# Small matmuls of a chunked recurrence that alternate between the two column halves of the PE array, with the matmuls kept in program order to the end of the kernel

## The chip, the cores and the metric

The kernel runs on one core of a Trainium2 chip. The metric is device time in microseconds (us). Before the change it is 338.93 us, the median of three runs (337.6 to 339.09).

## The reference

Two layers stand one behind the other. The first is a linear recurrence over 768 positions for 4 batches of 8 heads (32 values of a head, 16 values of state), computed in chunks; a chunk's output has a part from the chunk itself and a part from the state that it was handed, and the chunk makes the next state. The second layer takes the 3072 rows of 256 values, forms `(x w1) * (x w2)` with 1024 columns, and multiplies by `w3` and `w_out`.

```python
cum = np.cumsum(la, axis=-1)                      # la: log a of this chunk
L = np.exp(cum[:, :, :, None] - cum[:, :, None, :]) * causal
M = np.einsum('bhin,bhjn->bhij', Cc, Bc) * L
y = M @ x + np.einsum('bhin,bhnd->bhid', Cc, state) * np.exp(cum)[..., None]
state = exp(sum(la)) * state + (B * x * decay_from_j).sum(positions)
...
a = x @ w1; b = x @ w2
out = (a * b @ w3) @ w_out
```

## The kernel before

**Chunks and slabs.** The positions are cut into 16 chunks of 48; two chunks make a slab, so there are eight slabs. A slab of all batches is 384 rows for the second layer. `w3 w_out` is formed once, at the start, into `WO`.

**One chunk of the recurrence** (`chunk(c)`) has four kinds of matmul, two heads to each. `decay` (tile `pd`) forms the exponents, ScalarE takes their exponential into `R`. `cb` (tile `pc`) forms the product of B and C: for the first slab two matmuls per half `hf` of the head pairs from float32 operands (tile `gf`), for every other slab 16 small bfloat16 matmuls per `hf`, 32 per chunk, of 96 rows, 64 columns and 48 streamed columns. `weigh` on VectorE multiplies `pc` into `R`. `Mx` (tile `py`) multiplies x and the state by `R`: 16 float32 matmuls of 128 rows, 64 columns and 64 streamed columns. The profile records a float32 matmul as two passes, so a `py` block is 32 passes, and a pass has its own weight load.

**Column halves.** The 64 columns of a small matmul lie either in PE columns 0 to 63 or in 64 to 127; which of them follows from the PSUM partitions that it writes (`64 * h2` in `cb`, `64 * pp` in `Mx`). Before the change the loop over the half is the outermost one: all matmuls of columns 0 to 63 first, then all of columns 64 to 127.

**After `Mx`** VectorE transposes the state out of `py` (`Z`), copies it with four small copies into the next chunk's operand `xe`, and ScalarE and VectorE write the outputs as two parts `xT` (high and low) for the second layer.

**The second layer** of a slab is eight tiles of `up` (tile `bank<-xT,w1..` and `w2..`: 12 matmuls with 384 streamed columns each), each followed by its gate: a copy on ScalarE, a product on VectorE (`gf`), a rounded copy on ScalarE (high part of `g`) and a difference on GpSimd (low part of `g`). Then come three groups of `down` (tile `bank<-woh,g` and `wol`: 24 matmuls with 256 streamed columns each, the eight tiles of `g` in turn, each with its high part twice and its low part last).

**What sets the order.** Slabs 0 and 1, the weights, and the chunks c0 to c5 are written out by hand in `PLAN`; there every instruction keeps the program's order. From slab 2 on (the loop at the end), `ordered[0]` is False and a scheduler decides, engine by engine; chunks c6 to c15 are formed there, two in each of the slabs 2 to 6, in four stages that are put behind the `up` tiles 0 to 3 (first chunk) and 4 to 7 (second chunk): `decay`, then `cb` and `weigh`, then `Mx`, then the steps after it.

Of the kernel before, what the change touches and what calls it, by code (L numbers as in the profile page):

```python
# [15 lines left out]
T = 48  # L16
# [4 lines left out]
PLAN = """  # L21
# [33 lines left out]
def kernel(  # L55
# [14 lines left out]
):  # L70
    """x, Bn, Bt, Ct, b0 and c0 as layouts() gives them, w3t with its columns first.
    The linear recurrence runs in chunks of T positions, two heads to a
    matmul.  The state rides along as N pseudo-positions in front of each
    chunk (their B rows are unit vectors, their x rows the state's rows), so
    one product M^T x gives the chunk's outputs with the carried part, and the
    columns B * decay beside M give the next state.  The layer (w3 w_out) is
    formed once.  float32 products of the layers go as hi + lo float32r parts, CB as
    sums over products of three bfloat16 parts."""
    nc = tc.nc
# [24 lines left out]

    # the start goes in the order of PLAN, engine by engine; the rest as it comes
    ordered = [True]

    def ins(i):
        return tc.keep_in_program_order(i) if ordered[0] else i

    def mm(*args, **kw):
        return ins(nc.tensor.matmul(*args, **kw))  # L112

# [14 lines left out]

# [1 line left out]
    # products of the two layers, by turns; before that the first slab's B^T  # L130
    # and C^T: rows (head pair of a half, n), columns (half, chunk, head
    # parity, ..), in C beside zeros for the other pairs' rows
    GF = const.tile([P, NGF, TOK], F32, name="gf")
# [14 lines left out]

    # exponent operands: rows 0..T-1 the causal mask, then per head parity three
    # parts of cum_i, then per head pair three parts of cum_j  # L150
    NG = NB * HP
# [13 lines left out]

# [1 line left out]
    Q, SQ = P // (NB * H), a.shape[1]  # L167
# [47 lines left out]

# [1 line left out]
    NQ = P // N  # L217
    XW = [t.shape[2] // NQ for t in (Bt, Ct)]
    dparts = [[dram.tile([3, N, NQ * XW[w]], BF16, name=f"d{'bc'[w]}{k}") for k in range(NSL)] for w in range(2)]

    # slots: B parts 0 1 2, 0 1, 0 against C parts 2 1 0, 1 0, 0; C's parts lie
    # in the order 2 1 0
    RUNS = ((0, 3, 0, 0), (3, 2, 0, 1), (5, 1, 0, 2))
# [61 lines left out]

# [1 line left out]
    xT = {}  # L287

    def chunk(c):
# [27 lines left out]
        def cb(hf):  # L317
            pc = ps_at.tile([P, 512], F32, name="pc", tag="at")
            pcv = v["pc", hf] = pc[:, :half * T].rearrange("p (g s) -> p g s", s=T)
            for h2 in range(2):  # L320
                if sl == 0:
                    kk = (hf * CPS + cc) * 2 + h2
                    mm(pcv[64 * h2:64 * h2 + 64].rearrange("p g s -> p (g s)"), B0[:, kk],
                       C0[:, kk].rearrange("p g t -> p (g t)"), start=True, stop=True)
                else:
                    for g in range(half):
                        mm(pcv[64 * h2:64 * h2 + 64, g], BP[:, hf * half + g, cc, h2], CP[:, hf * half + g, cc, h2],
                           start=True, stop=True)

# [4 lines left out]
        @step("Mx")  # L334
        def _():
            if cc == 0:
                xT[sl] = [work.tile([P, KT, NB, SL], F32R, name=f"xT{i}") for i in range(2)]
            py = ps_at.tile([P, 512], F32, name="py", tag="at")
            v["py"] = py.rearrange("p (k b m) -> p k b m", k=KT, b=NB)
            for pp in range(2):  # L340
                for kt in range(KT):
                    for b in range(NB):
                        hp = 2 * kt + pp
                        mm(v["py"][64 * pp:64 * pp + 64, kt, b, :], xe[:, b * HP + hp], v["R"][:, b * HP + hp, :],
                           start=True, stop=True)
# [35 lines left out]

# [1 line left out]
    W12 = [[const.tile([P, KT, DF], F32R, name=f"w{i}{p}") for p in "hl"] for i in (1, 2)]  # L383
    WO = [const.tile([P, FT, DM], F32R, name=f"wo{p}") for p in "hl"]

    def from_f64(name, src, dst=None):
        """Brings src, [P, 2 k] words of float64 in DRAM, low word first, to
        float32.  Scaled by 2^-112 as a float32, a high word has float32's
        exponent at its exponent's low end; magnitudes under 2^-119 vanish
        there.  Then the high word takes the low word's top byte as its lowest  # L390
        byte, to bring sign and last bits in one step."""
        v = {}

        @task(name + ".D")
        def _():
            v["st"] = work.tile([P, 2 * GR], F32, name="st", bufs=4)
            load(v["st"].bitcast(U32).rearrange("p (f k) -> p f k", f=src.shape[1]), src)
            v["wh"] = v["st"].rearrange("p (k two) -> p k two", two=2)[:, :, 1]

        @task(name + ".A")  # L400
        def _():
            v["mag"] = work.tile([P, GR], F32, name="mag", bufs=4)
            if name + ".A" in ON_VECTOR:
                ins(nc.vector.tensor_scalar(v["mag"], v["wh"], 2.0 ** -112, None, ALU.mult))  # L404
            else:
                ins(nc.scalar.activation(v["mag"], v["wh"], AF.Copy, scale=2.0 ** -112))

        @task(name + ".Y")
        def _():
            b = v["st"].bitcast(U8).rearrange("p (k e) -> p k e", e=8)  # L410
            (vcopy if name + ".Y" in ON_VECTOR else acopy)(b[:, :, 4], b[:, :, 3])

        @task(name + ".L")
        def _():
            w = v["wh"].bitcast(I32)
            ins(nc.vector.tensor_scalar(w, w, 5, 7 - 2 ** 31, ALU.arith_shift_right, ALU.bitwise_and))  # L416

        @task(name + ".S")
        def _():
            mi = v["mag"].bitcast(U32)  # L420
            to = mi if dst is None else dst.bitcast(U32)
            ins(nc.vector.scalar_tensor_tensor(to, mi, 3, v["wh"].bitcast(U32),  # L422
                                               ALU.logical_shift_left, ALU.bitwise_or))
        return v
# [11 lines left out]

    # the first WHOLE tiles of (w3 w_out)'s inner dimension go as float32 products
    WHOLE = 2
# [19 lines left out]
    def w3_item(j):  # L458
# [11 lines left out]
        @task(f"v{j}.M")  # L470
        def _():
            for b in range(f0 // 2, (f0 + NF) // 2):
                if b not in opened:
                    # the bank holds two accumulators: a product of zeros opens both
                    opened.add(b)
                    mm(bank[b], zero[:, 0:P], zero, start=True, stop=False)
            left[j % 2] -= 1
            for f in range(NF):
                ft = f0 + f
                fs = slice(f * P, (f + 1) * P)  # L480
                if kt < WHOLE:
                    pairs = [(v["mag"][:, fs], wof[:, kt])]
                else:
                    pairs = [(v["tr"][:, l, fs], wos[:, kt - WHOLE, r]) for l, r in ((0, 0), (0, 1), (1, 0))]
                for k, (l, r) in enumerate(pairs):
                    mm(bank[ft // 2][:, ft % 2, :], l, r, start=False,
                       stop=(left[j % 2] == 0 and k == len(pairs) - 1 and ft % 2 == 1))
# [11 lines left out]

# [1 line left out]
    turn = [0]  # L501
# [7 lines left out]
    def up(sl, ft):  # L509
        """(x w1) * (x w2) of one slab, one tile of columns"""  # L510
        hi, lo = [t.rearrange("p k b s -> p k (b s)") for t in xT[sl]]
# [60 lines left out]

# [1 line left out]
    for c in range(2 * CPS, 3 * CPS):  # L574
# [25 lines left out]
    def keep_clock(n):  # L600
        """products of zeros, for a tensor engine that would lose its clock waiting"""
        for _ in range(n):
# [61 lines left out]
def layouts(x, a, B, C):  # L664
    """a as [(quarter of the positions, head parity, batch, head pair), positions];
    x as [chunk, head parity, t, (batch, head pair, d beside zeros)]; B as [slab, (head
    parity, n's unit rows and t), (chunk, batch, head pair, n)]; B^T (behind
    unit columns) and C^T as [slab, n, (batch, head pair, chunk, head parity,
    t)]"""
    import numpy as np  # L670
# [18 lines left out]

    # the first slab's once more, as [(head pair of a half, n), (half, chunk, head parity, ..)]  # L690
    b0, c0 = [t[0].reshape(N, 2, G // 2, CPS, 2, -1).transpose(2, 0, 1, 3, 4, 5).reshape(N * G // 2, -1) for t in (bt, ct)]
# [36 lines left out]
```

## Time and profile before

| what | value |
|---|---|
| three runs | 337.6, 338.93, 339.09 us |
| span of the profiled execution, first to last instruction | 336.5 us |
| granted TensorE clock, mean over the core | 0.985 |
| TensorE (PE) busy | 306.7 us, 91% |
| VectorE (DVE), ScalarE (ACT), GpSimd (POOL) busy | 164.8, 153.1, 139.3 us |

The profile is of a further execution, whose span alone is known; the median of the runs is 2.4 us above it. In the profile PE is the matmul side of TensorE, PEld its weight loads, SPq the queue that issues DMAs. A row of the timeline gives the start, the length from the first start to the last end, engine, line, what is written from what, and how many instructions were merged; a bracket gives idle time ahead of them and what ended it. Matmuls are pipelined, so each record is longer than the distance to the next start. Since every matmul is issued through the helper `mm`, all of them have one line, L112, and are told apart by their tiles.

### The profile page before, as it was taken

Reading aid. Unit: us, or ns where it says so; the run is one execution under the profiler, and the core shown is the slowest. Engines: PE = TensorE matmul, PEld = TensorE weight load, DVE = VectorE, ACT = ScalarE, POOL = GpSimd, SP = SyncE. Lnnn points to the kernel's source line nnn. Section 1 sums busy time; section 2 is a strip of 40 time slices with the busy share of each in tenths; the row PEclk is TensorE's granted clock in tenths of the full one; section 3 lists DMA queues with packets and bytes.
Section 4 is the critical chain, followed back from the end, with each engine's and each line's share of the span. In section 5 each row is a group of like instructions: output and inputs, shape, how many; then the busy total and the mean of one; then the engine's idle time right before and its main releaser. Section 6 shows DMA issues by size and latency. Waiting matters only on the chain.

```text
span 336.5 us, 6661 instructions
## 1 busy us (share of the span) xinstructions
PE 306.7 (91%) x2569; PEld 276.7 (82%) x2571; DVE 164.8 (49%) x292; ACT 153.1 (45%) x290; POOL 139.3 (41%) x157
## 2 busy tenths in 40 slices
PE   8695896976868999899999999999999999999995
PEld 3452786965857998889999899889988998999995
DVE  3869989999987523634313340344035302510210
ACT  4466687866574644454214431433144223422421
POOL 8037278836856664243213421343043304420440
PEclk9799799799999999999999999999999999999999
DMA  7599699775969695753840294029302920001001
GB/s 210 186 285 266 213 261 231 231 226 159 299 155 190 209 208 185 237 150 85 174 101 20 52 179 95 19 82 179 76 8 60 196 56 3 2 2 47 0 2 47
DMA packets 26255, 45.31 MB, mean 135 GB/s; under 512 B 7600, under 2 KB 17200, under 8 KB 25552
## 3 DMA queue, kind: packets, MB, share of 16 engines
q1 hardware_dynamic: 26224, 44.89, 51.8%
q8 instruction: 20, 0.33, 0.4%
q14 instruction: 11, 0.09, 0.1%
HBM read 36.77 MB, written 8.11 MB: 133 GB/s over the span
## 4 chain that ended last, share of the span: by engine, by line
PE 63%; DMA 13%; DVE 13%; ACT 4%; issue 4%; POOL 2%; SPq 1%; ACTq 0%; DVEq 0%; POOLq 0%
PE bank L112 52%; PE py L112 7%; DMA raw<-in_Ct_dram 4%; DMA xe<-in_x_dram 4%; DVE mag L422 3%; PE pc L112 3%; DMA st<-in_w_out_dram 2%; DMA raw<-in_Bt_dram 2%; DVE st L124 2%; DVE st L416 2%; DVE xe L124 2%; ACT st L118 2%; DMA st<-in_w3t_dram 1%; PE pd L112 1%; POOL part L127 1%
## 5 line engine op out<-in xcount | busy, mean ns | idle before, releaser
L127 POOL TENSOR_TENSOR g<-gf,g 128x384 fp32r<-128x384 f32 x64 | 66.6, 1043 | 96.2 <-ACT g L118 96.0
L121 DVE TENSOR_TENSOR gf<-gf,bank 128x384 f32<-128x384 f32 x48 | 26.6, 554 | 95.7 <-PE bank L112 84.7
L112 PE MATMUL bank<-woh,g 128*128 128x256 f32 x384 | 71.6, 285 | 0.3 <-ACT gf L118 0.3
L112 PEld LDWEIGHTS bank<-woh,g 128*128 128x128 f32 x384 | 60.4, 191 | 0.7 <-ACT gf L118 0.5
L118 ACT COPY gf<-bank 128x384 f32<-128x384 f32 (+1 forms) x72 | 31.5, 443 | 51.1 <-PE bank L112 51.1
L118 ACT CAST g<-gf 128x384 fp32r<-128x384 f32 x64 | 32.9, 515 | 47.4 <-DVE gf L121 47.3
L112 PE MATMUL bank<-wol,g 128*128 128x256 f32 x192 | 53.4, 283 | 0.0
L112 PE MATMUL bank<-xT,w1h 128*128 128x384 f32 x192 | 51.6, 350 | 0.0
L112 PE MATMUL bank<-xT,w2h 128*128 128x384 f32 x192 | 51.0, 347 | 0.0
L112 PEld LDWEIGHTS bank<-wol,g 128*128 128x128 f32 x192 | 36.4, 192 | 0.0
L112 PEld LDWEIGHTS py<-R,xe 128*64 128x64 f32 x512 | 28.7, 139 | 8.3 <-DVE R L121 2.7
L112 PE MATMUL py<-R,xe 128*64 128x64 f32 x512 | 31.0, 227 | 4.3 <-DVE R L121 2.3
L112 PEld LDWEIGHTS bank<-xT,w1h 128*128 128x128 f32 x192 | 33.8, 188 | 1.1
L112 PEld LDWEIGHTS bank<-xT,w2h 128*128 128x128 f32 x192 | 33.4, 188 | 1.0
L112 PE MATMUL bank<-xT,w2l 128*128 128x384 f32 x96 | 32.4, 337 | 0.0
L127 POOL TENSOR_TENSOR R<-bn,R 128x128 f32<-128x128 f32 x32 | 14.8, 482 | 42.2 <-issue 35.6
L112 PE MATMUL bank<-xT,w1l 128*128 128x384 f32 x96 | 32.1, 335 | 0.0
L118 ACT COPY st<-st 128x512 uint8<-128x512 uint8 x20 | 27.5, 1374 | 8.8 <-DVE mag L404 8.6
L422 DVE SCALAR_TENSOR_TENSOR mag<-mag,st 128x512 uint32<-128x512 uint32 x27 | 30.0, 1109 | 0.9
L112 PE MATMUL bank<-wos,tr 128*128 128x256 f32 x144 | 20.8, 292 | 6.9 <-POOL tr L127 4.4
L118 ACT CAST part<-raw 128x512 bf16<-128x512 f32 (+1 forms) x28 | 16.1, 576 | 21.8 <-DMA raw<-in_Ct_dram 14.4
L112 PEld LDWEIGHTS bank<-wos,tr 128*128 128x128 f32 x144 | 18.4, 190 | 8.8 <-POOL tr L127 5.7
(77 smaller groups left out, 441.7 us busy)
## 6 DMA issues: line engine op xcount, KB each, us to landing
st<-in_w3t_dram SPq DMA_DIRECT2D x16, 512.0 KB
xe<-in_x_dram SPq DMA_DIRECT2D x32, 192.0 KB
st<-in_w_dram SPq DMA_DIRECT2D x8, 512.0 KB
db<-part SPq DMA_DIRECT2D x7, 384.0 KB
bp<-db SPq DMA_DIRECT2D x7, 384.0 KB
st<-in_w_out_dram SPq DMA_DIRECT2D x4, 512.0 KB
bn<-in_Bn_dram SPq DMA_DIRECT2D x8, 256.0 KB
dc<-part SPq DMA_DIRECT2D x7, 288.0 KB
```

The lines of the kernel that those rows point to most:

```text
L112: return ins(nc.tensor.matmul(*args, **kw))
L118: return ins(nc.scalar.copy(*args))
L121: return ins(nc.vector.tensor_tensor(*args))
L124: return ins(nc.vector.tensor_copy(*args))
L127: return ins(nc.gpsimd.tensor_tensor(*args))
L416: ins(nc.vector.tensor_scalar(w, w, 5, 7 - 2 ** 31, ALU.arith_shift_right, ALU.bitwise_and))
L422: ins(nc.vector.scalar_tensor_tensor(to, mi, 3, v["wh"].bitcast(U32), ALU.logical_shift_left, ALU.bitwise_or))
```

## The change

The helper `mm` keeps matmuls in program order everywhere, not only where `PLAN` rules. In `cb` (for all slabs but the first) and in `Mx` the loop over the column half becomes the innermost one, so consecutive small matmuls write to columns 0 to 63 and 64 to 127 by turns. The number of matmuls, their operands and what they add up are as before. Comments are removed, which moves no instruction; lines behind `cb` stand one further down.

```diff
     def mm(*args, **kw):
-        return ins(nc.tensor.matmul(*args, **kw))
+        return tc.keep_in_program_order(nc.tensor.matmul(*args, **kw))
...
-            for h2 in range(2):
-                if sl == 0:
+            if sl == 0:
+                for h2 in range(2):
                     kk = (hf * CPS + cc) * 2 + h2
                     mm(pcv[64 * h2:64 * h2 + 64].rearrange("p g s -> p (g s)"), B0[:, kk],
                        C0[:, kk].rearrange("p g t -> p (g t)"), start=True, stop=True)
-                else:
-                    for g in range(half):
-                        mm(pcv[64 * h2:64 * h2 + 64, g], BP[:, hf * half + g, cc, h2], CP[:, hf * half + g, cc, h2],
-                           start=True, stop=True)
+                return
+            for g in range(half):
+                for h2 in range(2):
+                    mm(pcv[64 * h2:64 * h2 + 64, g], BP[:, hf * half + g, cc, h2], CP[:, hf * half + g, cc, h2],
+                       start=True, stop=True)
...
-            for pp in range(2):
-                for kt in range(KT):
-                    for b in range(NB):
+            for kt in range(KT):
+                for b in range(NB):
+                    for pp in range(2):
                         hp = 2 * kt + pp
                         mm(v["py"][64 * pp:64 * pp + 64, kt, b, :], xe[:, b * HP + hp], v["R"][:, b * HP + hp, :],
                            start=True, stop=True)
```

The order within `cb` and `Mx` is read from these loops. Where the blocks stand among the other matmuls is another matter, since the scheduler had moved them. The first place is on PE in slab 2, around the `pc` matmuls of chunk c6; `bank_109<-..w1` and `bank_110<-..w2` are the two halves of the `up` tile 1:

```order
@@ -744,8 +744,4 @@
 L112 MATMUL bank_109<-xT_1385,w1h 128x384
 L112 MATMUL bank_109<-xT_1384,w1l 128x384
-L112 LDWEIGHTS bp
-L112 MATMUL pc<-cp,bp 64x48
-L112 LDWEIGHTS bp
-L112 MATMUL pc<-cp,bp 64x48
 L112 MATMUL bank_110<-xT_1384,w2h 128x384
 L112 MATMUL bank_110<-xT_1385,w2h 128x384
```

Before, two `pc` matmuls stood between the two halves of an `up` tile and the other 30 behind it (in every second chunk it is five and 27); now the 32 stand together behind the whole tile.

The second place is on PE in the same slab, around the `py` block of c6; `bank_109` and `bank_110` are here the two halves of the `up` tile 3, and the rows that lie between the two pieces are the rest of these:

```order
@@ -826,4 +826,5 @@
 L112 MATMUL bank_112<-xT_1385,w2h 128x384
 L112 MATMUL bank_112<-xT_1384,w2l 128x384
+L112 MATMUL py<-R,xe_79 64x64 x16
 L112 MATMUL bank_109<-xT_1384,w1h 128x384
 L112 MATMUL bank_109<-xT_1385,w1h 128x384
@@ -835,5 +836,4 @@
 L112 MATMUL bank_110<-xT_1385,w2h 128x384
 L112 MATMUL bank_110<-xT_1384,w2l 128x384
-L112 MATMUL py<-R,xe_79 64x64 x16
 L112 MATMUL bank_110<-xT_1384,w2h 128x384
```

The block moves ahead by nine matmuls: from the middle of the second half of the tile 3 (or 7, for a slab's second chunk) to the end of the tile before it.

The third place is on PE at the start of the `down` matmuls of slab 2; `bank_111` and `bank_112` hold the first and the second group:

```order
@@ -970,4 +970,6 @@
 L112 MATMUL bank_111<-woh,g 128x256 x2
 L112 MATMUL bank_111<-wol,g 128x256
+L112 MATMUL bank_111<-woh,g 128x256 x2
+L112 MATMUL bank_111<-wol,g 128x256
 L112 MATMUL bank_111<-woh,g 128x256
 L112 MATMUL bank_112<-woh,g 128x256
```

Before, the scheduler put most of the second group ahead of the first group's last three matmuls, which need the last tile of `g`; now the first group is finished before the second begins. On VectorE the four copies into `xe` now stand together, ahead of the gate's product of the `up` tile that follows `py`; before, that product stood between the second and the third copy.

## The prediction

> **What bounds the kernel now.** I read the page first, then the engines' busy time cut at the seams of the slabs (`up` of slab 2 starts at 143.28 us and of slab 3 at 176.06).
>
> ```profile
> span 336.5 us, 6661 instructions
> PE 306.7 (91%) x2569; PEld 276.7 (82%) x2571; DVE 164.8 (49%) x292; ACT 153.1 (45%) x290; POOL 139.3 (41%) x157
> ...
> 0.00:143.28 143.28, 117.20 (x901) 98.56 (x904) 108.37 (x168) 87.31 (x143) 82.36 (x88) 0.96 0.79 220
> 143.28:176.06 32.78, 32.78 (x301) 30.46 (x300) 11.29 (x26) 11.91 (x28) 10.55 (x13) 1.00 0.56 128
> 274.40:307.20 32.80, 32.80 (x302) 30.59 (x302) 8.91 (x19) 11.19 (x25) 9.57 (x12) 1.00 0.05 14
> ```
>
> The columns behind the window's length are PE, PEld, DVE, ACT and POOL, then the clock, the DMA share and GB/s. There are two regimes. From slab 2 on PE is busy for all of each 32.8 us at full clock, the other engines for a third of it: what PE saves there is time saved. Ahead of 143.28 PE is idle for 26 us, and the chain of waits shows who leads at the seam:
>
> ```profile
> 132.67 3.55 DMA raw<-in_Ct_dram
> 136.32 0.51 ACT part L118
> 136.83 0.55 ACT gf L118 x2
> 137.43 8.23 PE bank L112 x60
> ...
> 135.22 1.90 PE L112 MATMUL py<-R,xe 128*64 128x64 f32 x32 [1.17 <-DVE xe L124]
> 142.86 0.56 DVE L121 TENSOR_TENSOR xT<-py,xT 128x384 fp32r<-128x384 f32 x1
> 143.28 0.63 PE L112 MATMUL bank<-xT,w1h 128*128 128x384 f32 x2
> ```
>
> A load lands at 136.22, ScalarE casts it, copies two banks free, and only then, at 137.43, PE goes on; VectorE finishes the low part of `xT` at 143.42, and `up` of slab 2, which begins at 143.28, needs it for its second matmul. So in chunks c0 to c5 a shorter `py` or `pc` mostly makes PE wait longer. I put them at zero, with 1.5 us either way for loads that now start at other times.
>
> **What the change removes: `py`.** The 16 matmuls are 32 passes.
>
> ```profile
> 218.59 1.90 PE L112 MATMUL py<-R,xe 128*64 128x64 f32 x32
> 220.42 0.62 PE L112 MATMUL bank<-xT,w2h 128*128 128x384 f32 x2
> ...
> 218.70 0.69 PE L112 MATMUL py<-R,xe 128*64 128x64 f32 x9
> ...
> 143.28:336.50 193.22, 19.00 (x320) 17.61 (x320) 9.77 (x20) 4.79 (x10) 1.00 0.32 71
> ...
> L112 PE MATMUL py<-R,xe x512: 221/222/335, 28.1 to 298.0; 128*64 128x64 f32 x171
> ```
>
> The third row is a stretch in which only columns 0 to 63 work: nine passes in 0.69 us, each 0.222 long, so one starts every (0.69 - 0.222) / 8 = 0.059 us. If the two halves ran strictly one behind the other, the block would last 31 x 0.059 + 0.222 = 2.05; it lasts 1.90, so a little overlap exists where the halves meet. That the halves can run together for long is shown by the first slab's `pc`, whose two halves stand close to each other already:
>
> ```profile
> 21.32 1.51 PE L112 MATMUL pc<-gf 128*64 128x384 f32 x8
> L112 PE MATMUL pc<-gf x16: 486/486/538, 21.3 to 30.1; 128*64 128x384 f32 x16
> ...
> 29.55 0.54 PE L112 MATMUL pc<-gf 128*64 128x384 f32 x1
> 29.60 0.34 PE L112 MATMUL py<-R,xe 128*64 128x64 f32 x3
> ```
>
> Eight passes of six times the streamed columns of a `py` pass, each 0.486 long, take 1.51: as one row they would start (1.51 - 0.486) / 7 = 0.146 apart, which for 384 columns is too fast beside 0.059 for 64; as two rows of four they start (1.51 - 0.486) / 3 = 0.34 apart, six times 0.057. So they are two rows. And at 29.55 a pass of columns 0 to 63 starts although three passes of `py`, in the other half and ahead of it in the program, start only at 29.60: the engine lets a half go on while the other is queued. Before, it reaches the other half only when the first has nearly drained.
>
> With the halves by turns a `py` block is two rows of 16 side by side: 15 x 0.059 + 0.222 = 1.11. That saves 1.90 - 1.11 = 0.79 a block. Bounds: nothing, if the halves don't overlap in this order, and 0.85, if the pitch falls to 0.055. I take 0.79, since the first slab's rows show full overlap.
>
> **`pc` put together.** In c6 to c15 the 32 matmuls stand in two places.
>
> ```profile
> 211.95 0.51 PE L112 MATMUL bank<-xT,w1h 128*128 128x384 f32 x2
> 212.30 0.34 PE L112 MATMUL bank<-xT,w1l 128*128 128x384 f32 x1
> 212.57 0.24 PE L112 MATMUL pc<-cp,bp 96*64 96x48 bf16 x2
> 212.74 0.62 PE L112 MATMUL bank<-xT,w2h 128*128 128x384 f32 x2
> ...
> 213.99 0.83 PE L112 MATMUL pc<-cp,bp 96*64 96x48 bf16 x30
> 214.75 0.62 PE L112 MATMUL bank<-xT,w1h 128*128 128x384 f32 x2
> ...
> 56.60 0.58 PE L112 MATMUL pc<-cp,bp 96*64 96x48 bf16 x16
> L112 PE MATMUL pc<-cp,bp x448: 183/189/248, 56.6 to 292.3; 96*64 96x48 bf16 x150
> ```
>
> Two `up` matmuls start (0.51 - 0.34) = 0.17 apart. Without the two `pc` matmuls the next would have started at 212.30 + 0.17 = 212.47; it starts at 212.74, and its pair lasts 0.62 and not 0.51. So the visit costs 0.27 + 0.11 = 0.38, of which the two matmuls, at the (0.83 - 0.189) / 29 = 0.022 each of the long block, are 0.04. One visit fewer saves 0.34 a chunk. The number of visits for `py` and `pd` stays.
>
> **`pc` by turns.** At 0.022 a matmul the halves already overlap in part: the block of 16 has 0.026. Bounds: 0, if 0.022 is what the engine can issue with a weight load each, and 32 x (0.022 - 0.013) = 0.29, if each half alone had 0.026. I take the middle, 0.15. The Trainium skill, "TensorE: Matmul & The Clock Gate" (section "Wait — 56ns, not 53.3ns?"), says that starts never come closer than about 25 ns; by it these turns would bring nothing and the forecast would be 1.5 us higher. The trace's 0.022 already lies under that, so I don't take it as a floor.
>
> **What it costs: program order.** Where the scheduler no longer fills a wait, PE stands. `py` comes nine matmuls earlier and needs `weigh`:
>
> ```profile
> 214.64 1.01 DVE L121 TENSOR_TENSOR R<-pc,R 128x384 f32<-128x384 f32 x2
> ```
>
> This ends at 215.65, 1.7 behind the start of `pc` at 213.99. In the new order `pc` (about 0.6 with its exit), a tile of `up` (12 x 0.174 = 2.1) and two changes lie between, 2.8 at least: `py` doesn't wait. The first `down` group does get near a wait, at its 24th matmul, which needs the low part of the last `g`:
>
> ```profile
> 199.83 0.45 DVE L352 STREAM_TRANSPOSE Z<-py 128x256 f32<-128x256 f32 x1 [2.77 <-PE py L112]
> 200.93 0.55 DVE L121 TENSOR_TENSOR gf<-gf,bank 128x384 f32<-128x384 f32 x1
> 202.17 1.02 POOL L127 TENSOR_TENSOR g<-gf,g 128x384 fp32r<-128x384 f32 x1 [3.42 <-ACT g L118]
> 200.37 0.28 PE L112 MATMUL bank<-woh,g 128*128 128x256 f32 x1
> 200.49 0.28 PE L112 MATMUL bank<-wol,g 128*128 128x256 f32 x1
> 200.32 0.58 DVE L124 COPY xe<-Z 16x256 f32<-16x256 f32 x2
> ...
> 140.78 2.06 DVE L124 COPY xe<-Z 16x256 f32<-16x256 f32 x4
> 141.11 1.27 POOL L127 TENSOR_TENSOR part<-raw,part 128x512 bf16<-128x512 f32 x1 [2.14 <-ACT part L118]
> ```
>
> `down` starts at 200.37, its 24th matmul is due 23 x 0.12 later, at 203.13; the low part is ready at 203.19, hidden now because the scheduler put the second group's matmuls ahead. Afterwards the chain is: `py` ends, Z 0.45, four copies 1.16 together, the low part of `xT` 0.56, all ahead of the last gate's product on VectorE: 2.2, and as much time as the last `up` tile takes. Then product 0.55, ScalarE's high part 0.51, GpSimd's low part 1.02: 2.1 to 2.4 with the steps between, against 2.76 up to the 24th matmul, a slack of some 0.3. But GpSimd's low part of tile 6 now falls beside the copies, and at 140.78, beside a GpSimd instruction, four copies took 2.06, 0.9 more. Two of the four beside it would be 0.45 to 0.6 late; I count 0.3 left over for each of the slabs 2 to 6, 1.5 in all; the bounds are 0 and 0.9 each. ScalarE's and GpSimd's instructions keep their order otherwise; on SP the loads of `x` for c7 move ahead of the last load of C, which nothing needs soon.
>
> **The sum.** For each of c6 to c15: 0.79 + 0.34 + 0.15 = 1.28, ten times 12.8, less 1.5: 11.3. The span of 336.5 becomes 325.2; with the 2.4 us between it and the median of the runs, 338.93 - 11.3 = 327.6 us.
>
> **The rivals.**
>
> *Waits eat more of it.* All four copies are as slow in each slab as at 140.78 and no slack hides it: 0.9 for five slabs, 4.5 in place of 1.5: 330.6. For it speaks that row, against it the 0.58 for two at 200.32. Chance 0.12.
>
> *The halves do not run together in this order*: the change doesn't do what it is written for. Only the joined `pc` is left: 3.4 less 1.5 of waits, 337.0, which is about the bound of what is told from no change. Against it stand 21.32 and 29.55. Chance 0.05.
>
> *Slower: each change of half exposes its weight load.* In `py` the half changes with each of the 16 matmuls, in `pc` with each of 32; today that is once and three times.
>
> ```profile
> L112 PEld LDWEIGHTS py<-R,xe 128*64 128x64 f32 x512 | 28.7, 139 | 8.3 <-DVE R L121 2.7 <-issue 2.5 <-DVE mag L422 1.4
> L112 PEld LDWEIGHTS <-bp 96*64 96x64 bf16 x448 | 12.7, 113 | 8.1 <-issue 7.7
> ```
>
> Exposed in full that is 16 x 0.139 + 32 x 0.113 = 5.8 a chunk, ten times 58, less the 3.4: over 390 us. It decides from little: 0.34 / 48 = 7 ns a change would cost what the joined `pc` brings. Against it: 32 loads of 0.139 are 4.4 us and lie in a block of 1.90, so they hide even within one half. The Trainium skill states such a rule, "TensorE: Matmul & The Clock Gate" (section "The mechanism"): a weight load overlaps running matmuls only where the row groups differ, and both halves use the same rows here. By that rule the time goes this way; the block of 1.90 us disagrees with it already. Chance 0.03.
>
> **How the numbers follow.** 0.80 for the forecast. Its range: 324 with no waits, `pc` by turns at its upper bound and 1 us from the first chunks (12.8 + 1.4 + 1 = 15.2 saved, 323.7); 332 with the waits of the first rival and 1.5 us lost in the first chunks. That leaves out the other two rivals and the ends, under 2 in 10. A measurement of this kernel tells 0.5%, 1.7 us, from no change, so faster is anything under 337.2: 0.80 + 0.12 and a little of the third case, 0.93; within 0.5%: 0.04; slower: 0.03.
>
> **What would show it.** A `py` block of 32 passes with a length near 1.1; 32 `pc` in one row, near 0.65 to 0.75, and none of two or five; slabs of 32.8 - 2 x 1.28 + 0.3 = 30.5 us; PE's idle rows ahead of `down` naming POOL, if the waits are there; slab 2 still starting near 143. It is wrong if `py` stays near 1.9, if its weight loads spread out, or if slabs stay at 32.

## The result and the profile after

| | before | after |
|---|---|---|
| time, median (lowest to highest) of 4 runs each | 339.01 (337.6 to 339.43) us | 326.98 (325.63 to 327.66) us |
| ratio to before, 95% interval | | 0.963 [0.959, 0.968] |
| span of the profiled execution | 336.5 us | 325.9 us |
| granted TensorE clock, mean | 0.985 | 0.958 |

The forecast was 327.6 us with a range of 324 to 332, and a span of 325.2. Both came out within a microsecond. That it is so close is in part luck, since the errors of the terms go both ways; the experiments take the sum apart.

The page of after, and then the engines' busy time cut where `up` of slab 2, 3, 4, 5 and 6 starts (the columns are those of the same view of before):

```profile
span 325.9 us, 6663 instructions
PE 295.9 (91%) x2571; PEld 267.5 (82%) x2571; DVE 169.3 (52%) x292; ACT 153.8 (47%) x290; POOL 139.4 (43%) x157
```

```profile
0.00:144.19 144.19, 118.18 (x903) 98.98 (x904) 108.47 (x168) 87.35 (x144) 82.37 (x88) 0.91 0.78 221
144.19:174.66 30.47, 30.47 (x302) 28.67 (x301) 12.02 (x25) 11.89 (x27) 10.56 (x13) 1.00 0.56 132
205.28:235.90 30.62, 30.51 (x302) 28.67 (x301) 11.63 (x24) 11.45 (x25) 9.63 (x12) 1.00 0.46 95
266.53:296.79 30.26, 30.26 (x303) 28.62 (x301) 9.51 (x19) 11.36 (x25) 9.59 (x12) 1.00 0.06 16
```

The slabs went from 32.8 us to 30.3 to 30.6, at the same clock of 1.00 and with PE as full as before, so they bring the whole gain. The `up` of slab 7 starts at 296.79 now and started at 307.37 before (the cut at 307.20 in the forecast's window lies a little ahead of it): the five slabs took 164.09 us and take 152.60, 11.5 less. The stretch ahead of slab 2 is 0.9 longer, at a lower clock (0.91 for 0.96). The third row is the one slab shown in which PE isn't busy throughout: 30.62 with 30.51 of work.

The two blocks in slab 4 on PE's timeline, and the weight loads of `py` in the table of groups (behind the bar the busy time, 18.0 us, and the mean of one, 148 ns):

```profile
209.93 0.69 PE L112 MATMUL pc<-cp,bp 96*64 96x48 bf16 x32
...
212.83 1.15 PE L112 MATMUL py<-R,xe 128*64 128x64 f32 x32
```

```profile
L112 PEld LDWEIGHTS py<-R,xe 128*64 128x64 f32 x512 | 18.0, 148 | 10.1 <-DVE R L121 4.5 <-issue 2.5 <-DVE xe L124 1.8
```

`py` takes 1.15 where it took 1.90, all 32 `pc` stand in one row of 0.69, and the 32 loads of a `py` block, 4.7 us together by that mean, still run beside its matmuls. No load is exposed by the change of half.

The waits appear where the forecast had put them, in the first group of `down`. PE, VectorE and GpSimd in slab 3:

```profile
198.92 0.28 PE L112 MATMUL bank<-wol,g 128*128 128x256 f32 x1
199.31 0.50 PE L112 MATMUL bank<-woh,g 128*128 128x256 f32 x2
```

```profile
194.22 0.45 DVE L353 STREAM_TRANSPOSE Z<-py 128x256 f32<-128x256 f32 x1 [0.47 <-PE py L112]
194.71 1.79 DVE L124 COPY xe<-Z 16x256 f32<-16x256 f32 x4
194.71 0.90 DVE L124 COPY xe<-Z 16x256 f32<-16x256 f32 x1
196.53 0.56 DVE L121 TENSOR_TENSOR xT<-py,xT 128x384 fp32r<-128x384 f32 x1
197.00 0.54 DVE L121 TENSOR_TENSOR gf<-gf,bank 128x384 f32<-128x384 f32 x1
```

```profile
194.44 1.01 POOL L127 TENSOR_TENSOR g<-gf,g 128x384 fp32r<-128x384 f32 x1 [1.89 <-ACT g L118]
198.24 1.02 POOL L127 TENSOR_TENSOR g<-gf,g 128x384 fp32r<-128x384 f32 x1 [2.78 <-ACT g L118]
```

`down` matmuls start 0.12 apart; after the one at 198.92 the next comes 0.39 later, at 199.31, just as GpSimd's last low part ends (198.24 + 1.02 = 199.26). The chain behind it is the forecast's: GpSimd's low part of tile 6 (194.44 to 195.45) runs beside VectorE's four copies, these take 1.79, and the last gate's product stands behind them. The second row of copies is the first of the four alone, taken from a narrower window: it lasts 0.90, to 195.61, just behind the end of GpSimd's instruction, and the other three take 0.28 to 0.29 each. So the copies don't all slow down; one of them is held up. PE's rows carry no bracket for such short waits, since the pipelined records cover them; the distance of the starts shows them.

### The profile page after: what moved, and what is told of

It is laid out like the page before. It is cut to its first block, busy times and chain, and to the rows that moved or that the text cites. A ratio compares the mean times of both kernels' runs of the same rounds, so it can differ in the third digit from the quotient of the medians.

```text
span 325.9 us, 6663 instructions
## 1 busy us (share of the span) xinstructions
PE 295.9 (91%) x2571; PEld 267.5 (82%) x2571; DVE 169.3 (52%) x292; ACT 153.8 (47%) x290; POOL 139.4 (43%) x157
## 5 line engine op out<-in xcount | busy, mean ns | idle before, releaser
L112 PE MATMUL bank<-woh,g 128*128 128x256 f32 x384 | 73.6, 288 | 1.2 <-POOL g L127 0.6
L112 PEld LDWEIGHTS bank<-woh,g 128*128 128x128 f32 x384 | 61.3, 193 | 2.6 <-POOL g L127 1.9
L112 PE MATMUL bank<-wol,g 128*128 128x256 f32 x192 | 54.5, 284 | 0.0
L112 PE MATMUL bank<-xT,w1h 128*128 128x384 f32 x192 | 52.5, 354 | 0.0
L112 PE MATMUL bank<-xT,w2h 128*128 128x384 f32 x192 | 48.8, 335 | 0.0
L112 PEld LDWEIGHTS bank<-xT,w2h 128*128 128x128 f32 x192 | 34.8, 188 | 0.0
L112 PEld LDWEIGHTS bank<-xT,w1h 128*128 128x128 f32 x192 | 33.0, 188 | 1.6
L124 DVE COPY xe<-Z 16x256 f32<-16x256 f32 x60 | 27.3, 456 | 1.2
L112 PEld LDWEIGHTS py<-R,xe 128*64 128x64 f32 x512 | 18.0, 148 | 10.1 <-DVE R L121 4.5
L112 PE MATMUL py<-R,xe 128*64 128x64 f32 x512 | 20.3, 236 | 6.0 <-DVE R L121 4.1
```

The lines of the kernel that those rows point to most:

```text
L112: return tc.keep_in_program_order(nc.tensor.matmul(*args, **kw))
L124: return ins(nc.vector.tensor_copy(*args))
```

## The experiments

### The parts one by one

Four kernels, each the kernel before with one piece of the change. `order_only` changes the helper alone:

```diff
-        return ins(nc.tensor.matmul(*args, **kw))
+        return tc.keep_in_program_order(nc.tensor.matmul(*args, **kw))
```

> The kernel before with the helper mm keeping program order to the end; the loops over the column halves stay outermost. Theory A (the halves side by side carry the gain): only the joined pc is left, 10 x 0.34 = 3.4 us, less the waits ahead of the last product of the first down group, 1.7: span 336.5 - 1.7, time 1 to 3 us under the kernel before, py blocks still 1.90, pc blocks of 32 near 0.87. Rival (the program order itself carries the gain, by moving py and pc to better places): 8 us or more under the kernel before.

`py_only` changes the loops in `Mx` alone, `pc_only` those in `cb` alone, with the scheduler free as before:

```diff
-            for pp in range(2):
-                for kt in range(KT):
-                    for b in range(NB):
+            for kt in range(KT):
+                for b in range(NB):
+                    for pp in range(2):
```

> The kernel before with the halves by turns in Mx alone; the scheduler still orders matmuls from slab 2 on. Theory A: py blocks of 1.15 in place of 1.90 in all chunks, ten of them where PE is busy throughout: 7.5 us less there; pc still in two places; with up to 1 us lost ahead of slab 2: time 6.5 to 8 us under the kernel before. Rival (order carries the gain): under 3 us.

```diff
...
-                    for g in range(half):
-                        mm(...)
...
+            for g in range(half):
+                for h2 in range(2):
+                    mm(...)
```

> The kernel before with the halves by turns in cb alone, scheduler as before. Theory A: the pc block that follows a whole up tile shortens from 0.83 (30 matmuls) to near 0.66, at 16 ns a matmul; 0.14 a chunk, 1.4 us in ten chunks. If 22 ns a matmul were the floor of issuing a load and a matmul: no change in the block and in the time.

`early_only` has both loop changes, but only for the chunks c0 to c5 (the part in `Mx` is shown, that in `cb` is alike):

```diff
...
+            turns = [(kt, b, pp) for kt in range(KT) for b in range(NB) for pp in range(2)]
+            if not (c < 3 * CPS):
+                turns.sort(key=lambda t: t[2])
+            for kt, b, pp in turns:
```

> The kernel before with the halves by turns in cb and Mx of chunks c0 to c5 alone, scheduler as before from slab 2 on. Theory A: what these six chunks save is waited away, up of slab 2 starts at 143 to 144.3, time within 1 us of the kernel before, and rather later than before, since in the changed kernel the granted clock fell around the py of c5 and slab 2 began 0.9 later. Rival (the six chunks share in the gain as the others do): 4 to 5 us under the kernel before.

| kernel | time, us | ratio to before run beside it, 95% interval | steady slab, us |
|---|---|---|---|
| order_only | 336.25 | 0.991 [0.988, 0.994] | 32.26 |
| py_only | 332.07 | 0.978 [0.974, 0.982] | 31.26 |
| pc_only | 336.89 | 0.992 [0.990, 0.995] | 32.39 |
| early_only | 339.76 | 1.002 [0.999, 1.004] | as before |

The slabs are the windows from one `up` to the next (PE busy in all of each), and a slab of before is 32.79. First `order_only`, then `py_only`, then `pc_only`:

```profile
177.30:209.56 32.26, 32.26 (x302) 30.62 (x301) 10.69 (x24) 11.46 (x25) 9.55 (x12) 1.00 0.44 90
```

```profile
174.43:205.69 31.26, 31.26 (x302) 29.04 (x301) 10.59 (x24) 11.27 (x25) 9.58 (x12) 1.00 0.46 93
```

```profile
176.19:208.58 32.39, 32.39 (x302) 30.18 (x301) 10.59 (x24) 11.28 (x25) 9.57 (x12) 1.00 0.43 90
```

They save 0.53, 1.53 and 0.40 a slab, together 2.46, and 32.79 - 2.46 = 30.33: the three pieces add up, and after's 30.62 is that and 0.3 of waits. Per chunk it is 0.265 for `pc` put together, 0.765 for `py` by turns and 0.20 for `pc` by turns. The blocks on PE's timeline say the same. In `order_only`, the joined `pc` with its halves outermost, and `py` as it was; and the last two rows are VectorE's four copies and GpSimd's low part of tile 6, which ends where they begin:

```profile
214.21 0.89 PE L112 MATMUL pc<-cp,bp 96*64 96x48 bf16 x32
...
217.34 1.90 PE L112 MATMUL py<-R,xe 128*64 128x64 f32 x32
...
199.31 1.18 DVE L124 COPY xe<-Z 16x256 f32<-16x256 f32 x4
198.31 1.00 POOL L127 TENSOR_TENSOR g<-gf,g 128x384 fp32r<-128x384 f32 x1 [2.12 <-ACT g L118]
```

In `py_only` and `pc_only`:

```profile
215.29 1.15 PE L112 MATMUL py<-R,xe 128*64 128x64 f32 x32
```

```profile
213.54 0.66 PE L112 MATMUL pc<-cp,bp 96*64 96x48 bf16 x30
```

`py` goes from 1.90 to 1.15 with the halves by turns and stays at 1.90 without; the joined `pc` is 0.89 with the halves outermost and 0.69 by turns; in `pc_only`, where it isn't joined, the larger piece goes from 0.83 to 0.66. That `py` moved ahead by nine matmuls brings nothing: from the `up` matmul ahead of the block to the one behind it, start to start, it is 2.10 in before and in `order_only`. Keeping the order costs no wait by itself: in `order_only` the copies begin where GpSimd ends, take 1.18 and `down` runs through. The waits of after come from both together: with `py` 0.75 shorter the copies begin while GpSimd still works. `early_only` shows what the turns bring in c0 to c5: nothing that can be told.

### The waits taken away

`gate_first` is the kernel after, with program order kept also on VectorE around the last step: the gate's product, then the transpose of the state and its four copies (the edit of the product is shown, the other two are alike).

```diff
...
-        vtt(gs[sl, ft], gs[sl, ft], pab[1], ALU.mult)
+        tc.keep_in_program_order(nc.vector.tensor_tensor(gs[sl, ft], gs[sl, ft], pab[1], ALU.mult))
```

> The changed kernel with VectorE kept in program order for the gates' products and for Z and its four copies, so that the last gate's product of a slab stands ahead of the copies. Theory A (the four copies, slowed beside GpSimd, make the last low part of g late, and PE waits 0.37 us a slab ahead of the last down matmuls of the first group): these waits go, slabs of 30.25 in place of 30.6, span 1.5 to 2 us under the changed kernel's 325.9. Rival (GpSimd is late by its own queue): the waits stay and the span is the same.

It took 326.06 us, 0.962 [0.959, 0.966] of before. A slab, and VectorE and GpSimd at the end of its last `up` tile:

```profile
173.68:204.00 30.32, 30.32 (x302) 28.65 (x301) 11.76 (x24) 11.25 (x25) 9.89 (x12) 1.00 0.45 96
```

```profile
195.58 0.55 DVE L534 TENSOR_TENSOR gf<-gf,bank 128x384 f32<-128x384 f32 x1 [2.81 <-PE bank L112]
196.06 0.44 DVE L353 STREAM_TRANSPOSE Z<-py 128x256 f32<-128x256 f32 x1
196.53 1.90 DVE L359 COPY xe<-Z 16x256 f32<-16x256 f32 x4
...
196.83 1.16 POOL L127 TENSOR_TENSOR g<-gf,g 128x384 fp32r<-128x384 f32 x1 [2.36 <-ACT g L118]
```

With the product ahead of the copies GpSimd's last low part ends at 197.99, PE is busy in the whole slab, and the slab is 30.32 and not 30.62. The copies are as long as in after (1.90 beside GpSimd), but now nobody on PE waits for them. So the 0.3 is the wait, and its cause is the order on VectorE together with the copy that is held up. In the time of the whole kernel it is too little to be told: slabs 3, 4 and 5 lose 0.3 each and slab 2 0.2, 1.1 in all, and the intervals of the two ratios lie over each other.

### Do the turns cost something in the first chunks?

After starts slab 2 at 144.19, 0.9 later than before, at a lower clock. My theory was that the shorter blocks of c4 and c5 make PE wait there in several pieces, that the clock falls for it, and that this costs the 0.9. PE's timeline of after, and two windows, the one with the waits and the one behind it, show the fall:

```profile
132.50 0.39 PE L112 MATMUL bank<-woh,g 128*128 128x256 f32 x1 [0.26 <-ACT g L118]
...
133.60 0.39 PE L112 MATMUL bank<-woh,g 128*128 128x256 f32 x1 [0.60 <-POOL g L127]
135.15 0.33 PE L112 MATMUL py<-R,xe 128*64 128x64 f32 x2 [1.17 <-DVE xe L124]
135.77 1.93 PE L112 MATMUL py<-R,xe 128*64 128x64 f32 x30 [0.29 <-DVE xe L124]
```

```profile
132.43:135.84 3.41, 1.29 (x7) 0.75 (x9) 2.22 (x7) 1.56 (x5) 2.13 (x2) 1.00 0.83 237
135.84:139.25 3.41, 3.41 (x37) 3.29 (x38) 0.93 (x2) 1.60 (x6) 0.91 (x1) 0.50 0.76 221
```

Four waits of 0.26, 0.60, 1.17 and 0.29 within 3.5 us (132.24 to 135.77), then a clock of 0.50 for 3.41 us, and the `py` block of c5 takes 2.55 (135.15 to 137.70) in place of 1.15. Two kernels test whether the end of the kernel feels it. `late_only` is after with the halves outermost in c0 to c5, as they were:

```diff
...
+            if not (c >= 3 * CPS):
+                turns.sort(key=lambda t: t[2])
```

> The changed kernel with the halves outermost, as before, in chunks c0 to c5, and by turns from c6 on; program order to the end. Theory A (the turns bring nothing in c0 to c5 and cost 0.9 us there through the clock): up of slab 2 starts at 143.3 and not 144.2, the granted clock is back at 0.985, slabs of 30.6, span 325.0. Rival (the first chunks bring their share): span 2 to 4 us longer than the changed kernel's.

`zeros_c5` fills the wait ahead of `py` of c5 with eight matmuls of zeros:

```diff
+            if c == 5:
+                for _ in range(8):
+                    mm(py, zero[:, 0:P], zero, start=True, stop=True)
```

> The changed kernel with eight matmuls of zeros into the py tile of c5 ahead of its products, while PE waits for xe. Theory A (PE's waits of 0.6 and 1.2 us there let the granted clock fall to half, so that py of c5 takes 2.5 us and the matmuls after it run slow): py of c5 takes 1.15, clock stays at 1.0 from 130 us on, slab 2 starts at 143.3 to 143.5, span 325.0 to 325.2. Rival (the clock falls whatever PE does there, or the loads set slab 2's start): start at 144.2 as in the changed kernel.

`late_only` took 327.35 us (0.965 [0.962, 0.968]) and has the same span as after, 325.9, at a clock of 0.974; `zeros_c5` took 330.49 (0.973 [0.970, 0.977]), span 328.0. The seam to slab 2 on PE, with VectorE's low part of `xT`, in `late_only`:

```profile
143.45 0.34 PE L112 MATMUL bank<-xT,w1h 128*128 128x384 f32 x1
144.21 0.44 PE L112 MATMUL bank<-xT,w1h 128*128 128x384 f32 x1 [0.42 <-DVE xT L121]
...
143.60 0.56 DVE L121 TENSOR_TENSOR xT<-py,xT 128x384 fp32r<-128x384 f32 x1
```

and in `zeros_c5`, PE's rows and then VectorE's:

```profile
135.03 1.26 PE L112 MATMUL py<-R,xe 128*64 128x64 f32 x32
144.81 0.48 PE L112 MATMUL bank<-xT,w1h 128*128 128x384 f32 x1 [2.40 <-DVE xT L121]
...
140.67 0.45 DVE L356 STREAM_TRANSPOSE Z<-py 128x256 f32<-128x256 f32 x1 [1.06 <-ACT xT L118]
141.90 0.56 DVE L121 TENSOR_TENSOR raw<-raw,part 128x384 f32<-128x384 f32 x1 [0.79 <-ACT part L118]
142.38 1.79 DVE L124 COPY xe<-Z 16x256 f32<-16x256 f32 x4
144.20 0.56 DVE L121 TENSOR_TENSOR xT<-py,xT 128x384 fp32r<-128x384 f32 x1
```

In the time of the kernel the theory fails: `late_only` gains nothing over after. Its `py` of c5 keeps the clock, and yet slab 2's second matmul, the first that needs the low part of `xT`, waits until 144.21; its slab 3 starts at 174.61, after's at 174.66.

The profiles do show the price, though, from the start of `py` of c5 to the start of slab 2. In the six with a fall there (after, `order_only`, `early_only`, `gate_first`, `py_by_2`, `py_by_4`) that is 8.9 to 9.2 us, 9.04 in after. In five without one (`zeros_c5`, the twelfth, comes below) it is 7.6 to 8.1, 8.06 in before; in the four of them that come out at 7.6 or 7.7, PE then waits 0.2 to 0.4 for `xT`. So after's 0.9 arose here. `late_only` saves it, but its `py` of c5 starts at 135.76 where after's starts at 135.15, and that uses most of it up. Kernels whose matmuls are the same up to there reach this block at different times (135.22 in before, 135.88 in `order_only`); why is open.

The fall isn't bound to the turns either. Up to slab 2 `order_only` has the matmuls of before in the same order, and there the clock falls too; `pc_only` waits longer, 0.21, 0.60 and 1.17, and keeps it:

```profile
132.76:136.18 3.42, 1.75 (x15) 1.35 (x15) 2.26 (x6) 1.70 (x4) 2.21 (x3) 1.00 0.70 214
136.18:139.59 3.41, 3.41 (x34) 3.29 (x33) 1.28 (x3) 1.84 (x5) 0.91 (x1) 0.50 0.89 241
```

```profile
131.06:134.47 3.41, 2.57 (x18) 1.96 (x16) 1.66 (x3) 2.96 (x7) 3.02 (x4) 1.00 0.27 79
134.47:137.88 3.41, 2.27 (x35) 2.20 (x36) 2.63 (x7) 1.68 (x5) 0.67 (x2) 1.00 0.98 281
```

In all twelve profiles the clock changes only at points that lie 3.41 us or a whole multiple of it apart, and it is 1.00 or 0.50 between them; these windows, and the two of after, are cut at these points. In `order_only` both of its waits, 0.50 and 1.18, fall into one such step, PE is idle for 1.67 of it, and the next step has half the clock. In `pc_only` the waits are split by a point, 0.84 and 1.14, and the clock stays. Where the points lie differs from profile to profile. Over all twelve, no step at full clock with under 1.17 us of idle PE was followed by a fall, and every one with more than 1.88 was; in between the idle time alone doesn't decide.

`zeros_c5` keeps the clock (`py` of c5 in 1.26), and PE is at slab 2 at 142.08, two microseconds ahead of after, but `xT` is ready only at 144.76. It is not a clean test: on VectorE the instruction `raw<-raw,part`, which waits for ScalarE, stands between `Z` and the four copies here, and behind the low part of `xT` in every other kernel. The copies start 1.26 behind the end of `Z` and not at once, so up to half of the 2.40 of waiting is that. Behind the wait the clock falls in slab 2 itself, which lasts 34.67.

So with the clock kept the seam is VectorE's, as the forecast had it; with the fall PE comes later than `xT` (143.60 in after), and the seam is PE's. How often each happens, the few profiles don't tell. The mean clock of every run of `early_only`, 0.949 to 0.965, is below that of every run of before beside it, 0.967 to 0.983, and its time is that of before.

`late_only_gate_first` has both edits.

> Both edits together: turns from c6 on alone, and the gates' products ahead of the copies on VectorE. Theory A: both gains add up, span near 323.3, some 2.6 us under the changed kernel. It keeps VectorE's program order also in the first 143 us, where it was there already.

It took 326.38 us, 0.962 [0.959, 0.966]: like `gate_first` and after, and not to be told from either. Its span is 325.0 and not 323.3, since the part that `late_only` was to bring is not there.

### How often must the half change?

In after the half changes with every matmul, that is every two passes; before, every 16. `py_by_2` changes it every four passes, `py_by_4` every eight:

```diff
-            for kt in range(KT):
-                for b in range(NB):
-                    for pp in range(2):
+            for kt, b0 in [(k, j) for k in range(KT) for j in range(0, NB, 2)]:
+                for pp in range(2):
+                    for b in (b0, b0 + 1):
```

> The changed kernel with the half changing after every two matmuls (four passes) in Mx. Theory A (a half can hold three passes that wait while the engine goes on to the other half; measured: the second half's first pass starts when the first half has three passes left): nothing is lost, block 1.15 to 1.2, time as the changed kernel. Rival (only matmuls that stand next to each other overlap): block near 1.5, 3 us more.

```diff
-                for b in range(NB):
-                    for pp in range(2):
+                for pp in range(2):
+                    for b in range(NB):
```

> The changed kernel with the half changing after every four matmuls (eight passes) in Mx. Theory A (three passes can wait in a half): the second half starts when the first has three passes left, five pitches in, and so on: the last pass starts about 1.22 after the first, block 1.45 to 1.5, so 0.3 a chunk more, 3 us in ten chunks. Rival (overlap only at each change, by one pass): near 1.8, 6 us more. Rival (depth is no matter): 1.15.

`py_by_2` and `py_by_4` took 326.59 us (0.963 [0.958, 0.967]) and 330.97 us (0.974 [0.969, 0.978]). The `py` block of `py_by_2` and of `py_by_4`:

```profile
210.83 1.20 PE L112 MATMUL py<-R,xe 128*64 128x64 f32 x32
```

```profile
214.71 1.54 PE L112 MATMUL py<-R,xe 128*64 128x64 f32 x32
```

One half behind the other would be 2.05 by the forecast's working. With one change of half the block was 1.90, with three changes (`py_by_4`) it is 1.54: 0.15 to 0.17 a change, or three passes of 0.058 that overlap at each. With seven changes that would be more than two full rows allow, and the block is at its floor, 1.20 or 1.15. This fits an engine in which some three passes of a half can wait while it goes on to the other half; that picture is worked out from four blocks, and no run shows the queue itself.

## Why the prediction was right

**What bounds the kernel.** Right on both regimes. From slab 2 on each microsecond saved on PE was saved in the end: 11.5 us in five slabs. Ahead of it nothing was: `early_only` 1.002 of before, `late_only` the same span as after. The reason given, that VectorE leads at the seam, holds in the profiles that keep their clock and not in that of after: there PE leads, held up by a fall of the clock that the forecast doesn't have. Its 0.9 lies within the 1.5 allowed either way for loads; that the allowance covers it is luck.

**`py`, 0.79 a block: 0.765.** The rows of the first slab, where two rows of passes stood side by side, were the right ones. The block is 1.15 and not 1.11, since the third pass starts 0.1 behind the second and only from there on does each half start one each 0.058.

**`pc` put together, 0.34 a chunk: 0.265.** Oversized, by 0.75 us in all. The cost of a visit was read from one place, where two `pc` matmuls stood apart. They do cost 0.26 there, from the `up` matmul ahead to the one behind less a plain step of 0.17, but the two cost 0.06 and not 0.04 in the long block, and the rest of a slab's `up` matmuls gets shorter by 0.06 a chunk where the forecast had 0.11.

**`pc` by turns, 0.15: 0.20.** Undersized, by 0.5 us. The block of 32 lasts 0.69 with a last matmul of 0.19, so a matmul with its own weight load starts each (0.69 - 0.19) / 31 = 0.016 us; I had taken the middle between 0.022 and 0.013. The floor of about 25 ns that the Trainium skill gives in "TensorE: Matmul & The Clock Gate" (section "Wait — 56ns, not 53.3ns?") is not there between the halves: in this kernel two matmuls in different halves start about 3 ns apart and the next pair about 28 ns behind that. Within one half the starts stay about 31 ns apart, which is not under it.

**The waits, 0.3 for each of five slabs: 0.3 for three, 0.2 for one, none for one.** The place, the chain and the size were right: the copies take 1.79 beside GpSimd and 1.18 alone, and `gate_first`, which takes away their precedence, takes away the 0.3. That two of the four copies would be late was not right: one is, by 0.6, until GpSimd is done. Slab 6 was miscounted: the row of its window shows 19 VectorE instructions where slab 4 has 24, for its second chunk is the last one and hands no state on, so it has neither the transpose nor the four copies. That is 1.1 us in place of 1.5.

**The sum.** 7.65 + 2.65 + 2.0 - 1.1 = 11.2 by the experiments, 11.5 in the slabs of the two profiles, 11.3 forecast: the terms were off by 0.25 and 0.75 one way, by 0.5 and 0.4 the other. The span is 0.7 above the forecast's 325.2: slab 2 starts 0.9 later, and the slabs give 0.2 of that back. The time is 0.6 under the forecast: it lies 1.1 above its profiled span where that of before lay 2.4 above, so the distance of the two, carried over from before, was 1.3 too long. Most of that comes from setting a median beside the span of one execution. Each run also has its own span: kernels that keep all matmuls in order take 1.7 to 1.8 longer than it, those that don't 2.0 to 2.2, so 0.3 to 0.4 goes with the order, outside the span; why is open.

**The rivals.** Waits of 0.9 for each of five slabs: the copies reached 1.79, nearly the 2.06 of the row that spoke for it, and yet the wait was 0.3. Of the 0.6 that they lost, the other 0.3 fits the slack that the forecast counted. Halves that don't run together: refuted by 1.15 for 1.90. The exposed weight load, and with it the rule of the Trainium skill, "TensorE: Matmul & The Clock Gate" (section "The mechanism"), that a load overlaps running matmuls only where the row groups differ: all 32 loads of a `py` block use the same rows, and 4.7 us of them, by their mean, lie within 1.15. The trace disagrees with it here. (The same section also lets a load go ahead into a background weight buffer; no run shows whether that is what happens.)

## What to carry to other kernels

Where small matmuls use half of the PE array's columns, write the loop so that the half changes every one or two matmuls; that the work is even between the halves isn't enough if they come one behind the other. Price each part in the stretch where the engine that gets shorter is the one that is full, and put it at nothing where another engine leads, for there the saving becomes a wait, and a wait can cost clock. When a block gets shorter, look which instructions of other engines now fall beside each other, and count the slabs in which they really occur.

## What the hardware showed that was not expected

- Some three passes of one column half can wait while the engine starts passes of the other: blocks of 32 passes take 1.15, 1.20, 1.54 and 1.90 us with the half changing every 2, 4, 8 and 16 passes.
- A bfloat16 matmul of 48 columns with its own weight load costs 16 ns when the halves go by turns, and 22 ns with the halves outermost.
- The clock goes in steps of 3.41 us, at 1.00 or 0.50. Waits of 0.50 and 1.18 within one step brought the next one to 0.50; 0.21, 0.60 and 1.17, split over two steps, left it at 1.00. None of these waits was over 1.18.
- Four VectorE copies of 16 x 256 take 1.18 us alone and 1.79 to 2.06 beside a GpSimd instruction. The added time is in one copy, 0.90 in place of 0.28 in after, which ends just behind GpSimd's instruction.
